# Channel products of all mixers in float32r passes, outputs of six mixers by ScalarE and GpSimd

## The chip, the cores and the metric

The kernel runs on one core of a Trainium2 chip. The time is the device time of one execution in microseconds, a median of several; the profiled execution is one more, with its own time. PE is TensorE, DVE VectorE, ACT ScalarE, POOL GpSimd, SP the SyncE queue that issues the DMAs.

## The reference

Eight batches, eight heads of 64, 576 tokens. Attention keeps the 32 largest scores of each row; its output x (576 tokens by 512 channels) goes through a mixer with a channel product at its end.

```python
scores = scale * np.matmul(q, k.transpose(0, 1, 3, 2))
kth = np.partition(scores, -top_k, axis=-1)[..., -top_k:-top_k + 1]
scores = np.where(scores >= kth, scores, -1000000000.0)
attn = softmax(scores)                  # written out in the original
x = np.matmul(attn, v)                  # heads laid side by side: 512 channels
theta = x @ w_theta
zr, zi = x * np.cos(theta), x * np.sin(theta)
y = np.einsum('ts,bsd->btd', w_tok_r, zr) + np.einsum('ts,bsd->btd', w_tok_i, zi)
u = x + y
out = u + np.maximum(u @ w_ch, 0.0)
```

## The kernel before

**Attention.** The work is cut into 160 units: 8 batches, 4 pairs of heads, and per pair five blocks of queries (four of 128 tokens and a rest of 64, whose two heads share one tile). `scores` makes a unit's scores on PE (ps_score, L260; for full blocks the high and low float32r halves of k against a stacked q) and copies them by ACT into a buffer e (L269). `fold`, `pick` and `threshold` find the 32nd largest of 576 by DVE alone, with maxima of eight and replacements (L296 to L330); POOL keeps marks (L307, L333) and makes the limits (lim, L331). `penalize` is an ACT Relu into pen (L350) and a POOL subtraction (L352), `exponent` an ACT exponential (L362), `turn` PE transposes (pt L377, pq L387) with ACT copies out of PSUM (L379), `mix_values` the product with v (px, L407 and L410), `keep_values` an ACT copy into xt (L419).

**Mixer.** Each batch then has a mixer, a generator: normalization and transposes of x, theta (pth, L540), cosine and sine on ACT with POOL products (L567, L572) into tile z, then the two products that matter here. For each of 4 blocks of 128 channels and 2 halves of 288 tokens, nine token products are added up (py, L656) and DVE adds them to xt (`settle`, L632), which is then u. After that, for each of 4 blocks and 2 halves, four channel products (po, L688: `w_ch` tiles against u, plain float32, two PE instructions each), and `give` (L637) has DVE write max(po, 0) + u into the output block ot, which has one buffer (bufs=1, shared with a tile of the trigonometric part); after the second half SP stores it. Tile z has one buffer too, and so the next mixer's z waits until it is free.

**Passes.** A float32r tile holds the high part of a float32; the rest is kept in a second tile. `halve` makes both (ACT copy L423, subtraction L424 on the engine that it is given), and `passes` lists three products: high by high, high by low, low by high. The last mixer (batch 7, `split`) makes all its products in this way. The mixer of batch 6 (`parts`) does it for its channel products alone: its weights are halved by `halve_weights("ch")` (subtraction on DVE), u into tiles u_hi and u_lo (subtraction on DVE).

**Order.** `pipeline` writes the units one after the other, the steps of a unit in the order of the string PTUFKSTVMXZ, with scores three units ahead. The mixer of a batch runs beside the units of the next: `advance` lets its generator go on by a budget per unit, and each `yield` says what the piece before it cost (1 for a token or a float32 channel product). The last mixer has no units beside it. Instructions of an engine run in the order that the scheduler of the framework gives, with priorities from `later` and `high_priority`.

**Weights.** `widen_steps` turns the weights, given as 64-bit words, into float32, one job in each unit from the third on (step "M"): SP loads, three ACT operations, POOL products (L158, L160, L161). There are 17 jobs; the four of w_ch come last. The temporaries lie in the buffer of z (`room`). The pair of q and k after next is halved at the end of each pair of heads (POOL L213) and laid out by 12 SP copies.

## Time and profile before

| | |
|---|---|
| median of 3 runs | 1202.73 us (1202.6 to 1203.58) |
| profiled execution | 1202.05 us, its span 1200.3 us |
| granted TensorE clock, mean | 0.971 of full speed |
| busy PE / DVE / ACT / POOL | 1104.9 / 1102.9 / 1007.0 / 704.4 us |

The profile is of one execution. The span runs from its first to its last instruction; what lies around it is 1.75 us. A page gives shares and groups for the whole span; the chain of work that ended last tells which engine set the pace at each time, and windows cut busy times out of a stretch. A share of busy time is a mean over stages with different limits, so the rows below are taken from the stages in which the changed instructions stand.

### The profile page before, as it was taken

The page shows a single profiled execution, that of the slowest core. Times are in us where ns is not written, and L with a number is a line of the kernel's source. Part 1 is how long each engine was busy: PE and PEld are TensorE (multiplying, and loading weights), DVE is VectorE, ACT ScalarE, POOL GpSimd, SP SyncE. Part 2 cuts the span into 40 slices and gives each one's busy share as a digit, 9 for nine tenths or more (in the row PEclk, how much of TensorE's full clock was granted, in tenths as well). Part 3 has the DMA queues.
Part 4 walks back from the last instruction along what each step waited for, and adds up shares of the span by engine and source line. Part 5 has one row for each costly group of instructions (what it writes and reads, how often), then busy time and mean ns, then how long its engine had stood idle before and what let it go on. Part 6 is the DMA issues. An engine that isn't in the chain of part 4 may idle for free.

```text
span 1200.3 us, 23013 instructions
## 1 busy us (share of the span) xinstructions
PE 1104.9 (92%) x6325; PEld 839.3 (70%) x6325; DVE 1102.9 (92%) x4997; ACT 1007.0 (84%) x2029; POOL 704.4 (59%) x975
## 2 busy tenths in 40 slices
PE   4577768999999999999999999999999999999997
PEld 3454555777767876678757877677767777677887
DVE  7999999999999999999999999999999999997352
ACT  6899999998699988898798987899888987898560
POOL 5999765665365644666465653765545654656540
PEclk9867899999999999999999999999999999999999
DMA  6654432433432234332431334333332334200101
GB/s 172 189 165 129 118 82 73 101 92 81 132 80 71 58 107 112 100 93 71 125 94 46 81 102 121 76 96 90 95 91 69 92 102 122 72 13 7 41 1 43
DMA packets 80235, 108.24 MB, mean 90 GB/s; under 512 B 23136, under 2 KB 41824, under 8 KB 80096
## 3 DMA queue, kind: packets, MB, share of 16 engines
q1 hardware_dynamic: 80096, 106.67, 33.7%
q8 instruction: 53, 0.87, 0.3%
q14 instruction: 86, 0.70, 0.2%
HBM read 38.40 MB, written 9.44 MB: 40 GB/s over the span
## 4 chain that ended last, share of the span: by engine, by line
PE 49%; DVE 24%; ACT 17%; POOL 5%; issue 2%; DMA 2%; SPq 1%; ACTq 0%; DVEq 0%; POOLq 0%
PE py L656 15%; PE ps_score L260 6%; PE po L688 6%; PE pt L377 6%; PE px L407 6%; DVE lst L326 5%; PE pth L540 5%; DVE best L320 5%; DVE lst L304 4%; ACT e L362 4%; ACT pen L350 3%; ACT e L269 3%; DVE lo L297 2%; PE px L410 1%; DVE ps_score L296 1%
## 5 line engine op out<-in xcount | busy, mean ns | idle before, releaser
L352 POOL TENSOR_TENSOR e<-e,pen 128x576 f32<-128x576 f32 x288 | 366.3, 1287 | 105.1 <-ACT pen L350 104.0
L320 DVE MAX8 best<-lst 128x8 f32<-128x102 f32 (+3 forms) x1152 | 284.4, 288 | 8.4 <-POOL lim L331 7.8
L656 PE MATMUL py<-w,z 128*128 128x288 f32 x1008 | 267.9, 407 | 0.3 <-ACT xt L419 0.3
L362 ACT ACTIVATE e<-e,lim 128x576 f32<-128x576 f32 x288 | 225.1, 783 | 18.0 <-POOL e L352 17.2
L326 DVE MATCH_REPLACE8 lst<-best,lst 128x122 f32<-128x122 f32 (+2 forms) x864 | 231.4, 274 | 0.1
L350 ACT ACTIVATE pen<-e,lim 128x576 bf16<-128x576 f32 x288 | 210.3, 774 | 16.8 <-POOL lim L331 15.4
L260 PE MATMUL ps_score<-kh,q 128*128 128x288 f32 x512 | 184.5, 375 | 42.9 <-ACT e L269 21.9
L304 DVE MAX8 lst<-lo 128x8 f32<-128x72 f32 (+1 forms) x864 | 210.0, 294 | 0.1
L656 PEld LDWEIGHTS py<-w,z 128*128 128x128 f32 x1008 | 181.1, 191 | 40.2 <-ACT xt L419 1.2
L377 PE MATMUL pt<-ident,e 128*128 128x128 f32 x1152 | 181.0, 283 | 23.0 <-ACT e L362 14.9
L377 PEld LDWEIGHTS pt<-ident,e 128*128 128x128 f32 x1152 | 139.9, 144 | 63.4 <-ACT e L362 20.3
L269 ACT COPY e<-ps_score 128x576 f32<-128x576 f32 x256 | 161.8, 641 | 15.2 <-PE ps_score L260 14.7
L379 ACT COPY at<-pt 128x512 f32<-128x512 f32 x256 | 148.0, 586 | 16.1 <-PE pt L377 14.8
L260 PE MATMUL ps_score<-kl,q 128*128 128x288 f32 x512 | 150.7, 309 | 0.1
L407 PE MATMUL px<-at,vt 128*64 128x320 f32 (+1 forms) x1024 | 145.1, 428 | 1.7 <-ACT at L382 1.3
L260 PEld LDWEIGHTS ps_score<-kh,q 128*128 128x128 f32 x512 | 102.6, 200 | 62.4 <-ACT e L269 29.2
L297 DVE TENSOR_TENSOR lo<-ps_score,e 128x576 f32<-128x576 f32 (+1 forms) x160 | 109.9, 687 | 0.0
L407 PEld LDWEIGHTS px<-at,vt 128*64 128x64 f32 x1024 | 70.8, 143 | 55.5 <-issue 10.2
L260 PEld LDWEIGHTS ps_score<-kl,q 128*128 128x128 f32 x512 | 103.4, 202 | 6.7 <-issue 2.4
L540 PE MATMUL pth<-w,xt 128*128 128x512 f32 x224 | 103.2, 600 | 1.6 <-ACT xt L518 1.6
L213 POOL TENSOR_TENSOR raw<-raw,hi 128x1152 fp32r<-128x1152 f32 x31 | 82.1, 2649 | 31.8 <-ACT hi L212 28.1
L688 PE MATMUL po<-xt,w 128*128 128x288 f32 x384 | 100.4, 408 | 0.0
(138 smaller groups left out, 1918.0 us busy)
## 6 DMA issues: line engine op xcount, KB each, us to landing
kh<-hi SPq DMA_DIRECT2D x124, 144.0 KB, 2.8
kl<-raw SPq DMA_DIRECT2D x124, 144.0 KB, 2.7
raw<-in_qT_dram SPq DMA_DIRECT2D x31, 288.0 KB, 2.9
raw<-in_kT_dram SPq DMA_DIRECT2D x31, 288.0 KB, 3.2
q<-hi SPq DMA_DIRECT2D x62, 144.0 KB, 2.6
q<-raw SPq DMA_DIRECT2D x62, 144.0 KB, 2.8
vt<-in_v_dram SPq DMA_DIRECT2D x32, 256.0 KB, 3.3
out_dram<-ot SPq DMA_DIRECT2D x28, 288.0 KB, 2.2
```

The costliest lines, as they stand in the source:

```text
L260: nc.tensor.matmul(out[:, at : at + n], l, r, start=(i == 0), stop=(i == len(mm) - 1), skip_group_check=True)
L269: nc.scalar.copy(u.x[:, :, keys], u.ps[:, :, :HS])
L304: nc.vector.max(u.lst[:, w, QS + i * 8 : QS + i * 8 + 8], u.lo1[:, w, lo:hi])
L320: nc.vector.max(top[:, w, best], part[w])
L326: nc.vector.match_replace(out=rest, in_to_replace=top[:, w, best], in_values=part[w], imm_value=LOWEST)
L350: nc.scalar.activation(pen[:, w], u.x[:, w], AF.Relu, bias=u.lim[:, w, 0:1], scale=-STEEP)
L352: nc.gpsimd.tensor_sub(u.x[:, w], u.x[:, w], pen[:, w])
L362: nc.scalar.activation(u.x[:, w], u.x[:, w], AF.Exp, bias=u.lim[:, w, 1:2], scale=SCALE, accum_out=acc)
L377: fixed(nc.tensor.transpose(pt[:, c], e[:, w, at0 : at0 + P], ident))
L407: nc.tensor.matmul(px[sl, :n], pr["vt"][:, kb, sl], pr["at"][:, a, kb], start=(kb == 0), stop=False, skip_group_check=True)
L656: fill(nc.tensor.matmul(py[:, :HS], l, r, start=(i == 0), stop=(i == len(mm) - 1)))
L688: nc.tensor.matmul(po[:, :HS], l, r, start=(i == 0), stop=(i == len(mm) - 1))
```

## The change

It has four parts. Line numbers are those of the kernel before; the changed kernel's are some 13 to 31 higher (L688 becomes L719, L637 becomes L657 on ACT, L658 on POOL and L660 on DVE, L424 becomes L441, L352 becomes L369, L331 becomes L348, L158, L160 and L161 become L161, L163 and, for the channel weights, L167, L213 becomes L230).

1. The four channel weight tiles hold float32r high parts. `widen_steps` makes them by an ACT cast and takes the low part on POOL, and stores it by SP to a block in DRAM, `ch_low`, one job after.
2. The mixers of batches 0 to 6 make their channel products in passes. When all token products are written, u is cast into high parts on ACT and low parts on POOL, four blocks of 128x576 each, in a tile `halves` in the buffer of z; it is free when the last token product has read z. The low parts of the weights come by DMA from `ch_low`, 256 KB per block of 128 channels, into two places of that same tile: two loads ahead, the third and fourth when PE has finished the block that held the place. After the halving the generator yields 4, and 0.75 for every three passes. In the first block the last quarter of both halves' products comes at the end.
3. For batches 0 to 5 `give` becomes an ACT Relu from PSUM to ot and a POOL addition of u.
4. The last mixer loads the low parts of the channel weights too, in place of halving them; the subtractions of `halve_weights` are all on POOL.

```diff
@@ pools @@
+    away = ctx.enter_context(tc.tile_pool(name="away", bufs=1, space=bass.MemoryType.DRAM))
...
@@ widen_steps @@
-        for key, n, width in (("ch", NB, DM), ("th", NB, DM), ("tok", KB, S)):
-            wts[key] = [weight_tile(F32, width) for _ in range(n)]
+        for key, n, width, dtype in (("ch", NB, DM, F32R), ("th", NB, DM, F32), ("tok", KB, S, F32)):
+            wts[key] = [weight_tile(dtype, width) for _ in range(n)]
+        ch_low[0] = away.tile([NB, P, NB, P], F32, tag="ch", name="ch_low")
...
             nc.gpsimd.tensor_add(low, low, bits)
+            if dst.dtype == F32R:
+                c = i - (len(jobs) - NB)
+                whole = bits.bitcast(F32)
+                nc.gpsimd.tensor_mul(whole, low.bitcast(F32), sign)
+                halve(dst, whole, whole, nc.scalar.copy, nc.gpsimd.tensor_sub)
+                return lambda: nc.sync.dma_start(
+                    ch_low[0][:, :, c].rearrange("m p d -> p m d"), whole.rearrange("p (m d) -> p m d", d=P)
+                )
             nc.gpsimd.tensor_mul(dst, low.bitcast(F32), sign)
...
+        store = None
         for i in range(len(jobs)):
             if i + 1 < len(jobs):
                 fetch(i + 1)
-            convert(i)
+            done = convert(i)
+            if store:
+                store()
+            store = done
             yield
+        store()
+        yield
...
@@ halve_weights @@
-            halve(hi[c], lo[c], wts[key][c], nc.scalar.copy, nc.vector.tensor_sub if key == "ch" else nc.gpsimd.tensor_sub)
+            halve(hi[c], lo[c], wts[key][c], nc.scalar.copy, nc.gpsimd.tensor_sub)
...
@@ mixer @@
         if split:
             halve_weights("tok")
+            flat = two_blocks("e", NB, DM, "c_lo", EBUFS)
+            c_lo = [t.rearrange("p (k d) -> p k d", d=P) for t in flat]
+            for m in range(NB):
+                nc.sync.dma_start(c_lo[m].bitcast(F32), ch_low[0][m])
...
         def give(m, c, cs, ot, y):
-            nc.vector.scalar_tensor_tensor(ot[:, cs], y, 0.0, xt[:, m, cs], op0=ALU.max, op1=ALU.add)
+            if beside and bq < B - 2:
+                nc.scalar.activation(ot[:, cs], y, AF.Relu)
+                nc.gpsimd.tensor_add(ot[:, cs], ot[:, cs], xt[:, m, cs])
+            else:
+                nc.vector.scalar_tensor_tensor(ot[:, cs], y, 0.0, xt[:, m, cs], op0=ALU.max, op1=ALU.add)
...
-        if parts:
-            halve_weights("ch")
-            u_hi, u_lo = two_blocks("kh", NB, S, "u_hi"), two_blocks("q2", NB, S, "u_lo")
-            for p in range(NB):
-                halve(u_hi[p], u_lo[p], xt[:, p], nc.scalar.copy, nc.vector.tensor_sub)
+        if not split:
+            room = one.tile([P, ZB * DM], F32R, tag="z", name="halves")
+            u_hi, u_lo = [[room[:, (2 * m + i) * S : (2 * m + i + 1) * S] for m in range(NB)] for i in range(2)]
+            flat = [room[:, 2 * NB * S + i * DM : 2 * NB * S + i * DM + DM] for i in range(TEMPS)]
+            c_lo = [flat[m % TEMPS].rearrange("p (k d) -> p k d", d=P) for m in range(NB)]
+            for m in range(TEMPS):
+                nc.sync.dma_start(c_lo[m].bitcast(F32), ch_low[0][m])
+            for m in range(NB):
+                halve(u_hi[m], u_lo[m], xt[:, m], nc.scalar.copy, nc.gpsimd.tensor_sub)
+            yield 4
...
+            heads = ((0, range(NB)), (1, range(NB)))
+            if m == 0 and not split:
+                heads = ((0, range(NB - 1)), (1, range(NB - 1)), (0, (NB - 1,)), (1, (NB - 1,)))
+            for c, kbs in heads:
...
-                else:
-                    mm = [(wts["ch"][kb][:, ms], xt[:, kb, cs]) for kb in range(NB)]
...
+                for kb in kbs:
+                    mm = passes(wts["ch"][kb][:, ms], c_lo[m][:, kb], u_hi[kb][:, cs], u_lo[kb][:, cs])
+                    for i, (l, r) in enumerate(mm):
+                        pos = dict(start=(kb == 0 and i == 0), stop=(kb == NB - 1 and i == 2), skip_group_check=True)
+                        with later(M_TOK if split else 0):
+                            nc.tensor.matmul(po[:, :HS], l, r, **pos)
                     if not split:
-                        yield NB / len(mm)
+                        yield 0.75
                         flush()
...
+            if not split and m + TEMPS < NB:
+                nc.sync.dma_start(c_lo[m + TEMPS].bitcast(F32), ch_low[0][m + TEMPS])
```

**TensorE, first mixer, from the last token product to the channel products.** Names: ps_score are scores of the running units, pt and pq their transposes, px their products with v. Before, the first channel products follow on score products:

```order
L260 MATMUL ps_score<-kh,q_3115 128x288
L260 MATMUL ps_score<-kl,q_3115 128x288
L688 MATMUL po<-xt,w_236 128x288
L688 MATMUL po<-xt,w_237 128x288
L688 MATMUL po<-xt,w_238 128x288
L688 MATMUL po<-xt,w_239 128x288
L387 MATMUL pq<-ident,e 128x128 x2
L688 MATMUL po<-xt,w_236 128x288
L688 MATMUL po<-xt,w_237 128x288
L688 MATMUL po<-xt,w_238 128x288
L688 MATMUL po<-xt,w_239 128x288
L377 MATMUL pt<-ident,e 128x128 x4
```

After:

```order
L277 MATMUL ps_score<-kl,qpad_100 128x64
L404 MATMUL pq<-ident,e 128x128 x2
L719 MATMUL po<-halves,w_238 128x288 x2
L719 MATMUL po<-halves 128x288
L719 MATMUL po<-halves,w_239 128x288
L424 MATMUL px<-at_3322,vt 64x256 x8
L394 MATMUL pt<-ident,e 128x128 x4
L719 MATMUL po<-halves,w_239 128x288
L719 MATMUL po<-halves 128x288
L719 MATMUL po<-halves,w_240 128x288 x2
L719 MATMUL po<-halves 128x288
L719 MATMUL po<-halves,w_241 128x288
```

Each product with a float32 weight tile has become three with halves, and score products, transposes and px of the running units stand between them in other places. Between the last py and the first po there are now 17 score products, a set of four transposes (pt) and two single ones (pq).

**GpSimd, in the first mixer's channel products.** lim, marks and e are of the running units' thresholds and penalties. Before:

```order
L307 COPY marks<-lst 128x2x3
L331 TENSOR_TENSOR lim<-best,factors 128x4
L352 TENSOR_TENSOR e<-e,pen 128x576 x2
L333 COPY marks<-best 128x2x4
L331 TENSOR_TENSOR lim<-best,factors 128x4
L352 TENSOR_TENSOR e<-e,pen 128x576 x2
L307 COPY marks<-lst 128x2x3
L333 COPY marks<-best 128x2x4
```

After:

```order
L441 TENSOR_TENSOR halves<-xt,halves 128x576 x3
L350 COPY marks<-best 128x2x4
L369 TENSOR_TENSOR e<-e,pen 128x576
L348 TENSOR_TENSOR lim<-best,factors 128x4
L369 TENSOR_TENSOR e<-e,pen 128x576
L441 TENSOR_TENSOR halves<-xt,halves 128x576
L369 TENSOR_TENSOR e<-e,pen 128x576 x2
L324 COPY marks<-lst 128x2x3
L324 COPY marks<-lst 128x3
L658 TENSOR_TENSOR ot<-ot,xt 128x288 x4
L350 COPY marks<-best 128x2x4
L324 COPY marks<-lst 128x2x3
```

The four remainders of u stand among the units' work, and the additions of two output blocks (four halves) stand in a row ahead of the next unit's limits.

**GpSimd, at the start, where the channel weights are widened.** room holds the widening's temporaries, w_... are weight tiles, raw and hi the pair that is halved. Before, around the first two of the four blocks:

```order
L352 TENSOR_TENSOR e<-e,pen 128x576
L333 COPY marks<-best 128x2x4
L161 TENSOR_TENSOR w_236<-room 128x512
L158 TENSOR_TENSOR room<-room,eight 128x512
L307 COPY marks<-lst 128x2x3
L331 TENSOR_TENSOR lim<-best,factors 128x4
L160 TENSOR_TENSOR room<-room 128x512
L352 TENSOR_TENSOR e<-e,pen 128x576 x2
L333 COPY marks<-best 128x4
L161 TENSOR_TENSOR w_237<-room 128x512
L158 TENSOR_TENSOR room<-room,eight 128x512
```

After, around the remainders of the first two blocks:

```order
L163 TENSOR_TENSOR room<-room 128x512
L369 TENSOR_TENSOR e<-e,pen 128x576 x2
L350 COPY marks<-best 128x4
L441 TENSOR_TENSOR room<-room,w_238 128x512
L167 TENSOR_TENSOR room<-room 128x512
L230 TENSOR_TENSOR raw<-raw,hi 128x1152
L324 COPY marks<-lst 128x2x3
L350 COPY marks<-best 128x2x4
L348 TENSOR_TENSOR lim<-best,factors 128x2
L369 TENSOR_TENSOR e<-e,pen 128x576 x2
L441 TENSOR_TENSOR room<-room,w_239 128x512
```

A block's last product (L161 before) is now L167, and the remainder L441 has been added behind it; two of these stand ahead of and behind the pair's subtraction (L230).

## Rows read from the trace of the kernel before

**Rows 1.** The page, shares of busy time by engine and the span in 40 equal slices (30 us each; a digit is the busy share of a slice in tenths).

```profile
PE 1104.9 (92%) x6325; PEld 839.3 (70%) x6325; DVE 1102.9 (92%) x4997; ACT 1007.0 (84%) x2029; POOL 704.4 (59%) x975
...
PE   4577768999999999999999999999999999999997
...
DVE  7999999999999999999999999999999999997352
```

**Rows 2.** The page, the chain of work that ended last: shares of the span by engine, then by line.

```profile
PE 49%; DVE 24%; ACT 17%; POOL 5%; issue 2%; DMA 2%; SPq 1%; ACTq 0%; DVEq 0%; POOLq 0%
PE py L656 15%; PE ps_score L260 6%; PE po L688 6%; PE pt L377 6%; PE px L407 6%; DVE lst L326 5%; PE pth L540 5%; DVE best L320 5%; DVE lst L304 4%; ACT e L362 4%; ACT pen L350 3%; ACT e L269 3%; DVE lo L297 2%; PE px L410 1%; DVE ps_score L296 1%
```

**Rows 3.** The chain in order of time, from 1040 us to the end, where the last two mixers run; columns: start us, us, engine, tile and line, count of instructions.

```profile
1116.04 1.60 PE po L688 x12
...
1118.07 1.58 PE po L688 x12
...
1180.58 12.72 PE po L688 x96
```

**Rows 4.** The chain in order of time from 284 to 326 us, in the product stage of the first mixer (same columns); the first and the last of its eight groups of po, and one row of each of other products between them.

```profile
291.05 1.94 PE po L688 x8
...
302.14 0.53 PE ps_score L260 x4
...
305.57 0.22 PE pq L387 x2
...
314.62 1.94 PE po L688 x8
...
317.09 0.44 PE pt L377 x4
```

**Rows 5.** The chain in order of time from 425 to 462 us, in the product stage of the second mixer (same columns); the first and the last of the eight rows of ot.

```profile
433.01 0.36 DVE ot L637
...
454.53 0.36 DVE ot L637
```

**Rows 6.** Windows: stretch, its us, busy us of PE, PEld, DVE, ACT and POOL with the number of instructions, the clock granted to TensorE, the DMA share and GB/s. The first two lie in the widening at the start, the others around the product stages of the mixers of batches 0, 1, 4 and 5, four of six such windows; the two left out lie between these in every column of busy time.

```profile
90.00:120.00 30.00, 21.68 (x107) 14.88 (x103) 28.99 (x150) 27.20 (x55) 28.39 (x36) 0.73 0.45 129
120.00:150.00 30.00, 23.00 (x121) 16.02 (x122) 27.80 (x133) 27.62 (x59) 23.37 (x31) 0.81 0.46 118
290.00:324.00 34.00, 33.97 (x207) 27.50 (x207) 33.48 (x144) 27.46 (x56) 16.24 (x23) 1.00 0.35 100
430.00:464.00 34.00, 33.90 (x211) 26.71 (x209) 33.97 (x153) 28.84 (x60) 17.88 (x27) 1.00 0.43 118
...
830.00:864.00 34.00, 34.00 (x198) 27.02 (x197) 33.72 (x158) 26.75 (x56) 16.30 (x30) 1.00 0.37 103
970.00:1004.00 34.00, 34.00 (x200) 27.03 (x199) 33.28 (x157) 26.85 (x55) 17.44 (x29) 1.00 0.43 118
```

**Rows 7.** Groups of instructions by line with shapes kept apart: line, engine, operation, out<-in, shape, count | busy us, mean ns of one | idle time of the engine before them. The last line is from the view of one tile, u_lo: ns of one (least, median, most), first and last start.

```profile
L269 ACT COPY e<-ps_score 128x576 f32<-128x576 f32 x256 | 161.8, 641 | 15.2 <-PE ps_score L260 14.7
...
L567 POOL TENSOR_TENSOR z<-z 128x512 f32<-128x512 f32 x32 | 41.1, 1286 | 52.9 <-ACT z L566 49.6 <-DVE lo L299 3.2
...
L419 ACT COPY xt<-px 128x320 f32<-128x320 f32 x32 | 13.6, 424 | 12.5 <-PE px L410 12.5
...
L424 POOL TENSOR_TENSOR w<-w,w_hi 128x576 fp32r<-128x576 f32 x9 | 12.9, 1433 | 4.9 <-ACT w_hi L423 4.3
...
L419 ACT COPY xt<-px 128x256 f32<-128x256 f32 x32 | 11.6, 364 | 4.3 <-PE px L410 3.8
...
L572 POOL TENSOR_TENSOR whole<-end,whole 128x256 f32<-128x256 f32 x7 | 5.1, 732 | 2.4 <-ACT whole L564 2.4
...
L423 ACT CAST w_hi<-w 128x512 fp32r<-128x512 f32 x8 | 4.6, 624 | 0.2 <-PE pq L387 0.2
...
L423 ACT CAST u_hi<-xt 128x576 fp32r<-128x576 f32 x4 | 2.7, 666 | 0.0
...
L424 POOL TENSOR_TENSOR w_lo<-w,w_hi 128x512 fp32r<-128x512 f32 x1 | 1.3, 1305 | 0.1
...
L424 DVE TENSOR_TENSOR u_lo<-xt,u_hi x4: 734/748/759, 1068.5 to 1109.5; 128x576 fp32r<-128x576 f32 x4
```

**Rows 8.** The chain in order of time from 86 to 130 us (columns as in rows 3), where the channel weights are widened.

```profile
118.63 2.38 POOL raw L213
...
121.19 4.82 DMA room<-in_w_ch_dram
...
126.68 0.65 ACT room L157
127.33 0.53 ACT e L269
...
127.89 0.47 DVE ps_score L296
```

**Rows 9.** The page's DMA issues (out<-in, queue, count, KB each, median us from issue to landing), and one line of the view of waits (who waits <- for whom: us in all, times, longest us).

```profile
vt<-in_v_dram SPq DMA_DIRECT2D x32, 256.0 KB, 3.3
out_dram<-ot SPq DMA_DIRECT2D x28, 288.0 KB, 2.2
...
DVE ot L637 <- DMA out_dram<-ot: 7.1, 3, 2.6
```

More of the change, by code (lines that the diff above doesn't have):

```diff
@@ L116, in topk_attention_phase_mixer @@
     wts = {}
+    ch_low = [None]
     def weight_tile(dtype, width):
@@ L459, in share, with mixer @@
         return pace[0]
-    def mixer(bt, split=False, beside=False, parts=False):
+    def mixer(bt, split=False, beside=False):
         bq, xt, sums, sums_rem = bt["bq"], bt["xt"], bt["sums"], bt["sums_rem"]
@@ L762, in keep @@
                         done = B - 1 - u.bq
-                        running.append(mixer(u.batch, done == 0, done > 0, done == 1))
+                        running.append(mixer(u.batch, done == 0, done > 0))
             def ahead():
```

23 lines of the change are left out of this document (9 added, 14 removed).

## The prediction

> **What bounds the kernel now.** I read the shares of busy time and the slices first, then the chain of work that ended last, then windows of the stages that the change touches, then prices of single operations. The page shows two engines full at once: PE and DVE are both busy for 92% of the span and stand at nine tenths in nearly every slice between the start and the tail [rows 1]. So a gain needs both to get less work in the same stretch, and the chain has to say which of the two sets the pace where.
>
> By line, the chain gives the channel products (po, L688) 6%, some 72 us of 1200.3 [rows 2]. Of these, 2 x 12.7 = 25.4 us belong to the last two mixers, which already work in float32r passes (96 in 12.72 us [rows 3]). That leaves about 47 us for the six other mixers, and one such mixer's products are 8 groups of 1.94 us = 15.5 us [rows 4]. Three mixers make 46.6 us. So in three of the six mixers with float32 products PE is the chain through the whole product stage, as [rows 4] shows for the first; in the other three the chain runs through DVE, and there the operation that adds the output up (ot, L637) is on it with 0.36 us each time [rows 5]. The six windows of 34 us around the product stages say how little is between the two: PE is busy 33.9 to 34.0 us, DVE 33.3 to 34.0, ACT 26.8 to 28.8, POOL 16.2 to 17.9 [rows 6]. The clock granted to PE there is 1.00, so nothing hangs on it.
>
> **Channel products in passes.** A float32 product of 128x288 is two instructions; one accumulation of four products takes 1.94 us [rows 4]. The same accumulation in passes is 12 instructions, and 12 of them take 1.58 to 1.60 us in the seventh mixer [rows 3]; 96 in 12.72 us is 1.59 for 12. One group saves 1.94 - 1.59 = 0.35 us, a mixer with its 8 groups 2.8 us, six mixers 16.8 us of PE. On the chain only three mixers count: 3 x 8 x 0.35 = **-8.4 us**. The seventh mixer and the last keep their passes: 0.
>
> The rows make twelve passes 0.82 of the eight instructions. The Trainium skill (FP8 and Floating Point Precision, section TensorE Precision Notes) says that a true fp32 product is four passes through the array; three of four would be 0.75, 0.485 us a group, 11.6 us instead of 8.4, and would put the sum below at 1190.5 us. The rows decide here, as they hold the weight loads too.
>
> **Outputs by ScalarE and GpSimd.** DVE loses 8 operations in each of six mixers, at 0.36 us of its time each [rows 5]; in the three mixers where DVE is the chain this is 3 x 8 x 0.36 = **-8.6 us**. In the other three it is what lets the gain of PE stand: DVE there has 0.3 to 0.7 us to spare in a window [rows 6] and would be the bound at once if it kept them. ACT gains 8 operations of 128x288 per mixer; its copies out of PSUM take 364 ns at 256 columns and 424 at 320 [rows 7], so 0.39 us, 3.1 us a mixer. POOL gains 8 adds of 128x288; 732 ns at 256 columns and 1286 at 512 [rows 7] give about 0.80 us, 6.4 us a mixer.
>
> **Halving the moving operand.** Each of the first seven mixers now casts four blocks of 128x576 on ACT (666 ns, 2.7 us a mixer) and takes four remainders on POOL (1433 ns, 5.7 us a mixer) [rows 7]. The seventh mixer had both before, the remainders on DVE, and in addition halved the weights of the channel product once (4 x 0.62 us on ACT); what DVE loses there lies in the tail, where PE is the chain [rows 3], and counts 0. The remainder on DVE took 748 ns, on POOL 1433 [rows 7]. The Trainium skill (GPSIMD Engine Reference, section 4.1 Engine selection) advises VectorE for a two-input add, as GpSimd is about twice as slow; the rows agree (1.9 times). By that rule alone the outputs would stay on DVE, and the term of 8.6 us would fall away.
>
> **What the product stage then needs.** A window of 34 us should shrink to about 34 - 2.8 = 31.2 us. POOL needs 17 + 5.7 + 6.4 = 29 us of it. ACT needs 27.5 + 3.1 + 2.7 = 33.3 us by durations, but these overlap when work is dense: the copy of L269 lasts 641 ns [rows 7] and costs 0.53 on the chain [rows 8]. With 0.1 us off each of 56 old and 12 new operations ACT needs 26.5 us. So PE, DVE, ACT and POOL would all be 85 to 107% full. Bounds per mixer: nothing lost (ACT 26.5), or all but 0.7 us lost (ACT 33.3, so 2.1 us). Then there is the new wait at the start of the stage: the halves lie in the buffer of z, so the casts wait until the last product of py is done, then come a cast, a remainder and the load of the low weights (256 KB; the values of that size land after 3.3 us [rows 9]). Between the last py and the first po the order puts 17 score products, a set of transposes and two single ones, 17 x 0.13 + 0.44 + 0.22 = 2.9 us of PE by the steps of [rows 4]; the first remainder is there after some 0.7 + 1.4 us of work plus queueing, so PE waits 0 to 3 us. What waits behind PE's first product is the transposes and values of the running unit. I take 0.8 us a mixer for the stage and its start together, near the lower end, since ACT falls below the new window at the middle of its bounds (29.9 us): six mixers **+5 us**, bounds 0 and 17. For the seventh mixer, in the tail, the same start wait counts 0, since the casts stand beside px products and transposes of the last units; if that cover is gone it is up to 3 us.
>
> **Widening the weights at the start.** The four blocks of the channel weights get a cast on ACT (about 0.62 us) and a remainder on POOL (1305 ns [rows 7]) and a store each. Here POOL is busy 28.4 of 30 us between 90 and 120 us, then 23.4 of 30 [rows 6], and the chain runs on POOL until 121 us, then through the last load of these weights, ACT and DVE [rows 8]. In the order, two of the four remainders stand ahead of POOL's work for the pair and its subtractions there, two after it: 2 x 1.3 = 2.6 us on the chain, and the stores stand in SP's queue ahead of the pair's copies. I take **+3 us**, bounds 0 and 6 (all four, and ACT's casts).
>
> **DMA queue.** SP issues four loads and waits for PE with two of them; behind these stand the loads of a later pair and the outputs. The outputs already land 2.2 us after issue [rows 9]; these loads are ahead of their use by more than a unit, so I count 0 beyond the wait named above.
>
> **Sum.** The profiled execution took 1202.05 us (span 1200.3 and 1.75 around it); the median of the runs shown is 0.7 higher. -8.4 - 8.6 + 3 + 5 = -9.0 us: 1193.0 for an execution like the profiled one, **1193.7 us** as a median.
>
> **Rivals.**
> 1. Everything fits: ACT's operations overlap as its old ones do, the start waits are covered, POOL's extra work at the start falls into its idle 6.6 us. Then the whole 17 us come: 1185.7 us. For it: POOL has half of each product window free. Against it: ACT is at 80% of that window already.
> 2. ACT becomes the bound of the product stage without waiting: 33.3 us in place of 34, six times -0.7, plus 3 at the start: about 1201.5 us, no change that can be told (0.2%, 2.4 us, is about what a measurement of this kernel can tell).
> 3. Slower: the output block has one buffer, so ACT's Relu of the next block waits until the former block is added and has left. Two adds (1.6 us), an issue and 2.2 us to landing are about 4.1 us; in the order the third block's Relu stands three ACT operations (some 1.5 us) behind the second's, and POOL's adds stand ahead of a unit's limits and subtractions, so score copies, penalties and exponentials queue up behind them. PE needs 2 x 1.59 us for the products between and some 0.2 for what stands among them, 3.4 us, which leaves 0.7 us of waiting. With ACT at 33.3 us and two such waits a window is 34.7 us, six times +0.7, plus 3: 1210 us. It decides from about 0.7 us of waits at full durations, or 4 us at the middle ones. For it: DVE already met this wait three times, 7.1 us in all [rows 9].
> That the passes are not made is no rival: their pitch is in [rows 3].
>
> **Chances.** The forecast (1188 to 1200) 0.53, rival 1 (below 1188) 0.17, rival 2 0.13, rival 3 0.17. Faster by over 0.2%: 0.53 + 0.17 = 0.70; within it 0.13; slower 0.17. The range 1185 to 1207 leaves out about one in ten above (the dear half of rival 3) and some 5 in 100 below.
>
> **What would show it.** Right: twelve po passes in 1.6 us and no DVE operation of ot in the first six mixers; product windows some 2 us shorter; ACT and POOL at nine tenths there; the end of the widening some 3 us later. Wrong: PE or DVE waiting for ACT's score copies in the product stage for more than 2 us a mixer, Relu waiting for the output DMA, PE idle before the first po for more than 1 us a mixer, or the first mixer starting as early as before.

## The result and the profile after

The changed kernel takes 1208.59 us (median of 7 runs, 1207.01 to 1211.13) against 1202.6 us before (7 runs, 1199.83 to 1204.15): a ratio of 1.0057, 95% interval 1.0048 to 1.0067. It is slower by 6 us. The forecast was 1193.7, and the range ended at 1207.

The profiled execution after took 1211.13 us (span 1209.3), the slowest of the seven; the comparison below goes against the 1202.05 us of the profile before. The shares of the page answer to [rows 1] and the shares of the chain to [rows 2]:

```profile
PE 1103.1 (91%) x6517; PEld 849.5 (70%) x6517; DVE 1083.4 (90%) x4941; ACT 1032.5 (85%) x2101; POOL 780.7 (65%) x1055
...
PE 57%; ACT 16%; DVE 14%; DMA 6%; issue 3%; POOL 3%; SPq 1%; ACTq 0%; POOLq 0%; DVEq 0%
PE py L679 20%; PE ps_score L277 7%; PE pt L394 7%; PE px L424 7%; PE pth L555 5%; PE po L719 5%; DVE lst L343 3%; DVE best L337 3%; ACT pen L367 2%; DVE lst L321 2%; ACT e L379 2%; ACT e L286 2%; PE px L427 2%; DVE lo L314 1%; DMA halves<-ch_low 1%
```

DVE has lost 19.5 us of work; ACT has gained 25.5, POOL 76.3. What is new on the chain is DMA, 6% where it was 2%.

Where the time went is read from the token products, whose line names its first and last start. Of before and of after:

```profile
L656 PE MATMUL py<-w,z x1008: 403/406/511, 223.5 to 1106.6; 128*128 128x288 f32 x168
```

```profile
L679 PE MATMUL py<-w,z x1008: 403/406/510, 230.3 to 1112.0; 128*128 128x288 f32 x168
```

The first token product is 6.8 us late. From there I cut the span at each mixer's first token product: the **start** (up to the first of batch 0), the **loop** (six cycles, from there to the first of batch 6) and the **tail** (from there to the end of the last channel product). These are times of the timeline of PE, subtracted:

| us | start | loop | tail |
|---|---|---|---|
| before | 223.5 | 825.0 | 144.8 |
| after | 230.3 | 824.6 | 148.5 |

So the start lost 6.8 us, the loop gained 0.4 where 12 were forecast, and the tail lost 3.7; behind the last product 1.1 came back. The sum is 9.0, the difference of the spans.

**The loop.** Four windows of 34 us around product stages, batches 0, 1, 4 and 5, answer to [rows 6]:

```profile
297.00:331.00 34.00, 33.36 (x248) 28.30 (x247) 31.72 (x144) 28.51 (x62) 25.39 (x33) 1.00 0.44 133
435.00:469.00 34.00, 30.93 (x229) 26.46 (x230) 31.77 (x139) 30.07 (x67) 26.27 (x35) 1.00 0.47 136
848.00:882.00 34.00, 32.04 (x238) 27.52 (x238) 31.23 (x136) 29.27 (x63) 27.01 (x34) 1.00 0.44 127
986.00:1020.00 34.00, 32.84 (x251) 28.66 (x251) 32.21 (x151) 30.73 (x67) 27.75 (x37) 1.00 0.51 141
```

PE and DVE, both full before, now stand idle for 0.6 to 3.1 and 1.8 to 2.8 us, and ACT and POOL are not full either (28.5 to 30.7 and 25.4 to 27.8 of 34). Nobody is the bound: somebody waits. DVE waits for ACT's score copies, 21.7 us in the loop against 7.6 before (view of waits, 230 to 1045 us), a sign that the prediction had named. What ACT and PE wait for, the chain of the third mixer's product stage says, in order of time (start us, us, what):

```profile
572.76 2.89 DMA halves<-ch_low
...
585.01 3.17 PE po L719 x24
...
590.26 0.81 POOL ot L658
...
591.21 0.76 POOL ot L658
...
591.99 2.10 DMA out_dram<-ot
...
594.17 0.29 ACT ot L657
...
596.65 1.06 ACT hi L229
...
597.73 0.49 SPq L242
...
598.31 2.95 DMA out_dram<-ot
...
601.34 0.42 ACT ot L657
601.76 0.04 issue
601.81 2.37 PE px L424 x16
```

Twelve passes take 1.59 us (24 in 3.17), as [rows 3] said. Behind them stands a chain that was not there before: two additions on POOL, the store, its landing, and only then the next Relu, because ot has one buffer. The second time the store comes later still: on SP it stands behind a copy of the next pair, which waits for ACT's cast of that pair (596.65, then SP's queue at 597.73), and takes 2.95 us. The two additions of that block had ended at 597.35 (timeline of POOL), the store went out at 598.31. The Relu at 601.34 frees the accumulators, which px shares with po, and px of the running unit starts at once. The direct waits are small; the view of waits (us in all, times, longest):

```profile
POOL ot L658 <- ACT ot L657: 15.3, 8, 3.1
...
DVE ot L660 <- DMA out_dram<-ot: 7.0, 3, 2.5
...
ACT ot L657 <- DMA out_dram<-ot: 5.3, 5, 2.1
...
PE po L719 <- DMA halves<-ch_low: 4.1, 5, 1.3
```

The Relu's waits for the store lie in the mixers of batches 0, 2 and 4 alone (at 313 to 318, 594 to 601 and 869 to 877 us in the timeline of ACT); the chain runs through a store in the stages of batches 2 and 4. In the other three mixers no Relu waits for it. The wait for the first load of low weights is there in all six, 0.1 to 1.3 us of PE each. Before the change no output of the loop waited for the block: the three waits of [rows 9] lie in the tail, the first of them here.

```profile
1117.26 0.88 DVE L637 SCALAR_TENSOR_TENSOR ot<-po,xt 128x288 f32<-128x288 f32 x2 [2.64 <-DMA out_dram<-ot]
```

**The start.** The chain from 100 us on, which answers to [rows 8]:

```profile
121.83 8.56 DMA q<-raw
...
131.04 2.47 DMA ch_low<-room
...
133.60 0.69 ACT room L160
```

The copy of the pair lands 8.56 us after its issue. On SP the first store of low weights (120.61) and a load of raw weights (121.24) went out just ahead of it. Before, the copies were issued at the same time, with the load ahead of them but no store, and this copy landed after 4.7 us. Then a second store is on the chain, for which ACT's next widening waits.

That is not all of it. PE's four sets of sixteen products with v (px from at and vt) that started at 154.5, 167.8, 182.9 and 209.1 us before now start 3.8, 2.9, 4.5 and 7.4 us later. The delay grows in a stretch in which TensorE had a lower granted clock than before, and there the second set took 3.96 us in place of 2.37. A window, and that set in PE's timeline, of before and of after:

```profile
170.00:190.00 20.00, 15.76 (x88) 11.26 (x87) 20.00 (x92) 18.62 (x38) 13.88 (x18) 0.91 0.44 104
...
167.82 2.37 PE L407 MATMUL px<-at,vt 128*64 128x320 f32 x16 [0.64 <-ACT at L382]
```

```profile
170.00:190.00 20.00, 16.06 (x82) 10.69 (x83) 19.91 (x95) 18.52 (x40) 13.20 (x20) 0.74 0.36 85
...
170.74 3.96 PE L424 MATMUL px<-at,vt 128*64 128x320 f32 x16 [1.84 <-ACT at L399]
```

In this window the granted clock is 0.69 to 0.76 in the profiles of all six kernels that halve and store in the widening (the changed one, passes_alone, start_alone, tail_dve, tail_own, out_in_xt) and 0.83 to 0.94 in those of the other eleven. That the lower clock makes up the rest of the 6.8 us is not shown; it stands where the rest arises.

**The tail.** The seventh mixer's remainders (halves) stand in turn with POOL's halving of the last mixer's weights (w), all behind the last token product at 1112.0; the first channel product comes at 1116.25, and at 1124 the last quarter of the first block still waits for the last remainder:

```profile
1115.97 1.36 POOL halves L441
1117.33 1.38 POOL w L441
1118.70 2.75 POOL halves L441 x2
1121.45 1.25 POOL w L441
1122.70 1.39 POOL halves L441
1124.09 0.04 issue
1124.14 0.55 PE po L719 x2
```

### The profile page after: what moved, and what is told of

It reads as the page before. It is cut to its first block, busy times and chain, and to the rows that moved or that the text cites. A ratio compares the mean times of both kernels' runs of the same rounds, so it can differ in the third digit from the quotient of the medians.

```text
span 1209.3 us, 23519 instructions
## 1 busy us (share of the span) xinstructions
PE 1103.1 (91%) x6517; PEld 849.5 (70%) x6517; DVE 1083.4 (90%) x4941; ACT 1032.5 (85%) x2101; POOL 780.7 (65%) x1055
## 4 chain that ended last, share of the span: by engine, by line
PE 57%; ACT 16%; DVE 14%; DMA 6%; issue 3%; POOL 3%; SPq 1%; ACTq 0%; POOLq 0%; DVEq 0%
PE py L679 20%; PE ps_score L277 7%; PE pt L394 7%; PE px L424 7%; PE pth L555 5%; PE po L719 5%; DVE lst L343 3%; DVE best L337 3%; ACT pen L367 2%; DVE lst L321 2%; ACT e L379 2%; ACT e L286 2%; PE px L427 2%; DVE lo L314 1%; DMA halves<-ch_low 1%
## 5 line engine op out<-in xcount | busy, mean ns | idle before, releaser
L369 POOL TENSOR_TENSOR e<-e,pen 128x576 f32<-128x576 f32 x288 | 367.3, 1289 | 107.0 <-ACT pen L367 102.7
L277 PE MATMUL ps_score<-kl,q 128*128 128x288 f32 x512 | 153.2, 313 | 0.5 <-DMA kl<-raw 0.4
L424 PE MATMUL px<-at,vt 128*64 128x320 f32 (+1 forms) x1024 | 148.0, 428 | 5.1 <-ACT at L399 2.9
L424 PEld LDWEIGHTS px<-at,vt 128*64 128x64 f32 x1024 | 70.9, 142 | 61.3 <-issue 11.2
L719 PE MATMUL po<-halves,w 128*128 128x288 f32 x448 | 96.9, 304 | 2.9 <-POOL halves L441 1.9
L313 DVE TENSOR_TENSOR ps_score<-ps_score,e 128x288 f32<-128x288 f32 (+1 forms) x160 | 68.1, 426 | 33.3 <-ACT e L286 28.5
```

The lines of the kernel that those rows point to most:

```text
L277: nc.tensor.matmul(out[:, at : at + n], l, r, start=(i == 0), stop=(i == len(mm) - 1), skip_group_check=True)
L369: nc.gpsimd.tensor_sub(u.x[:, w], u.x[:, w], pen[:, w])
L424: nc.tensor.matmul(px[sl, :n], pr["vt"][:, kb, sl], pr["at"][:, a, kb], start=(kb == 0), stop=False, skip_group_check=True)
```

## The experiments

Every median stands with its ratio to the kernel before, taken in the same series, and the 95% interval. The table after them has start, loop and tail of each.

**Each part alone.** `gives_alone` is the kernel before with part 3 only:

```diff
+            if beside and bq < B - 2:
+                nc.scalar.activation(ot[:, cs], y, AF.Relu)
+                nc.gpsimd.tensor_add(ot[:, cs], ot[:, cs], xt[:, m, cs])
+            else:
                 nc.vector.scalar_tensor_tensor(ot[:, cs], y, 0.0, xt[:, m, cs], op0=ALU.max, op1=ALU.add)
```

> The kernel before with part 3 alone: Relu by ScalarE and addition by GpSimd for batches 0 to 5, float32 channel products, no halving. Theory A (the single output block makes the Relu wait for addition and landing, and the accumulators are held that long): PE needs two groups of 1.94 us and little else per block against a chain of two additions and a landing of about 4 us, so PE waits a little in most blocks: 1203 to 1208 us. Rival B (what hurts is how full ScalarE and GpSimd are, and they are not so full without the halving): 1200 to 1203 us, as DVE loses 8.6 us on the chain of three mixers, of which PE gives back most.

Measured: 1210.05 us, 1.0069 (1.0055 to 1.0084). Slower by itself, with float32 products and without the halving of six mixers. Beyond A's range, but on its side; the mechanism of A is not shown by it, as the trace has 1.6 us of Relus waiting for the store (three waits), and its loop is 7.5 us longer than before.

`passes_alone` is the changed kernel with all outputs by DVE:

```diff
-            if beside and bq < B - 2:
+            if False:
```

> The changed kernel with its outputs by VectorE as before: passes, halving, loads and the wider start stay. Theory A (start +6.8 us and tail +4.7 us are separate from the outputs; in the loop the wait for the first loads stays, the wait for the output block goes, and VectorE is the bound again): 1206 to 1211 us. Rival B (the outputs on ScalarE and GpSimd are the main cost): 1203 us or below.

Measured: 1219.54 us, 1.0157 (1.0134 to 1.0179). Neither. In the loop either half alone is worse than both: 832.5 us with the outputs, 839.0 with the passes, 824.6 with both. (As a median gives_alone is not to be told from the changed kernel, since it has no loss in start and tail.) The outputs on ACT and POOL aren't the main cost; they are what makes the passes bearable.

`start_alone` is the kernel before with this behind the last product of the widening of each channel weight block (cut to the lines that matter), and the store one job later, as in the change:

```diff
+            c = i - (len(jobs) - NB)
+            if c >= 0:
...
+                part = bits.bitcast(F32)
+                halve(spare[0][:, c % 2, :DM], part, dst, nc.scalar.copy, nc.gpsimd.tensor_sub)
+                return lambda: nc.sync.dma_start(
+                    ch_low[0][:, :, c].rearrange("m p d -> p m d"), part.rearrange("p (m d) -> p m d", d=P)
+                )
```

> The kernel before with the start's part alone: after each of the four channel weight blocks is widened, its high part is cast by ScalarE (into a spare buffer that nothing reads), the remainder taken by GpSimd and stored by SP one job later; nothing else is changed and nothing reads what was stored. Theory A (the start costs what weights_later gave back in the first 230 us): first token product 5 to 7 us late, 1207 to 1210 us. Rival B (the start costs little, and weights_later gained by the order that the scheduler made of the loop): first token product within 2 us, 1201 to 1204 us.

Measured: 1208.61 us, 1.0052 (1.0039 to 1.0066). Its token products start at 230.0 us, 6.5 late, and end 8.1 late; from the third cycle on the loop has the old order and the old times. A holds; the start alone is worth as much as the whole loss. The path is another one than in the changed kernel: here the copy of the pair landed 2.8 us after its issue, and on the chain stood the last load of raw weights, which went out at 124.93, behind the copies, and landed 3.2 us later than before. So the late copy is one way for the start to lose, not the cause that both share.

```profile
L675 PE MATMUL py<-w,z x1008: 403/406/510, 230.0 to 1114.7; 128*128 128x288 f32 x168
```

**The start mended.** `weights_later` widens the channel weights as before the change, but into a buffer of the scores, and halves and stores them in the units after (cut):

```diff
-            if dst.dtype == F32R:
...
+        for _ in range(WLATE):
+            yield
+        for c in range(NB):
+            whole = jobs[c - NB][0]
+            halve(wts["ch"][c], whole, whole, nc.scalar.copy, nc.gpsimd.tensor_sub)
+            nc.sync.dma_start(
+                ch_low[0][:, :, c].rearrange("m p d -> p m d"), whole.rearrange("p (m d) -> p m d", d=P)
+            )
+            yield
```

> The changed kernel with the four channel weight blocks widened as before (into a buffer of the scores) and halved in the units after, one per unit, so that the remainders and stores stand after the pair's subtraction and copies at 120 us. Theory A (the 6.8 us that the first token product is late come from these remainders and stores ahead of the pair's copies): 1202 to 1204 us, first token product at 224 to 226 us. Rival B (it is the amount of work of GpSimd and ScalarE ahead of the first mixer, wherever it stands): 1207 to 1209 us, first token product at 229 to 231 us.

Measured: 1198.51 us, 0.9974 (0.9962 to 0.9986), faster than before. The first token product is back at 224.6 us, as A said, but 10 us came and not 6: the loop, whose code is the same, is 9.8 us shorter as well. (5.7 and 9.8 are more than 10, as the profiled execution after was 2.5 us above its median and this one 2.9 below.) Its order differs from the changed kernel's in the first four cycles and is the same on every engine in the last two; most of the gain lies in the cycles of batches 1 and 2, which took 139.7 and 139.3 us after, 134.5 and 136.8 here. Its Relus wait 2.9 us for the store, in six waits of at most 0.7, where the changed kernel has 5.3 with 2.1 as the longest. What the one output block costs hangs on the order that the scheduler makes around it.

```profile
L681 PE MATMUL py<-w,z x1008: 403/406/510, 224.6 to 1096.6; 128*128 128x288 f32 x168
```

**The tail.** `tail_dve` puts the seventh mixer's four remainders back on DVE, nothing else:

```diff
-                halve(u_hi[m], u_lo[m], xt[:, m], nc.scalar.copy, nc.gpsimd.tensor_sub)
+                halve(u_hi[m], u_lo[m], xt[:, m], nc.scalar.copy, nc.gpsimd.tensor_sub if beside and bq < B - 2 else nc.vector.tensor_sub)
```

> The changed kernel with the four remainders of the seventh mixer's u on VectorE, as before the change; batches 0 to 5 keep GpSimd. Theory A (in the tail the remainders queue behind GpSimd's halving of the last mixer's weights and the first channel product waits for them, 7 us of which 4.7 stay to the end): 1204 to 1205 us. Rival B (the first products wait for the loads and for the casts as well, so that only the order of the waits changes): 1207 to 1209 us.

Measured: 1212.77 us, 1.0087 (1.0072 to 1.0101). Both theories fell: the tail grew by 8 us. The four subtractions took 12.75 us on DVE, beside POOL's halving of weights (ns of one: least, median, most; then the four in DVE's timeline and three of the subtractions in POOL's):

```profile
L441 DVE TENSOR_TENSOR halves<-xt,halves x4: 1765/1896/7421, 1110.0 to 1115.4; 128x576 fp32r<-128x576 f32 x4
...
1110.05 12.75 DVE L441 TENSOR_TENSOR halves<-xt,halves 128x576 fp32r<-128x576 f32 x4 [1.95 <-ACT halves L440]
...
1118.22 3.96 POOL L441 TENSOR_TENSOR w<-w,w_hi 128x576 fp32r<-128x576 f32 x3
```

`tail_own` gives that mixer's halves their old buffers and its remainders to DVE, and loads its low weights ahead of the token products (cut):

```diff
+        tail = beside and bq == B - 2
+        if tail:
+            flat = two_blocks("e", NB, DM, "early", EBUFS)
...
+        if tail:
+            u_hi, u_lo = two_blocks("kh", NB, S, "u_hi"), two_blocks("q2", NB, S, "u_lo")
+            for p in range(NB):
+                halve(u_hi[p], u_lo[p], xt[:, p], nc.scalar.copy, nc.vector.tensor_sub)
```

> The changed kernel with the seventh mixer's halves of u in buffers of their own (those of the pairs, as before the change), its remainders on VectorE, and its low weights loaded into buffers of the scores ahead of its token products; batches 0 to 5 and the start stay as in the change. Theory A (in the tail the casts, remainders and loads all stand behind the last token product because the halves share z, and this costs 7 us there): first channel product of that mixer within 1 us of the last token product, and 1203 to 1205 us. Rival B (the tail loses to something else, such as the loads of the last mixer or GpSimd): 1207 to 1210 us.

Measured: 1206.66 us, 1.0032 (1.0020 to 1.0045), between the two. The wait ahead of the products is gone (the first starts 3.2 us before the last token product ends, by the timeline of PE), but the tail still takes 148.1 us. `later_tail` has the edits of weights_later and of tail_own, as they stand above:

> The edits of weights_later and tail_own together. Theory A (start and tail are separate costs that add up): 1198.5 - 4 to 5 = 1193 to 1195 us. Rival B (whatever is gained in the tail is met by other waits there): 1197 to 1199 us.

Measured: 1197.68 us, 0.9959 (0.9946 to 0.9972); its interval overlaps that of weights_later. B: the tail keeps its loss.

**The output block.** `out_in_xt` is the changed kernel with two lines changed. With passes, u is read only as halves once they are made, so POOL adds in place and SP stores from xt; ot is free after the addition:

```diff
-                nc.gpsimd.tensor_add(ot[:, cs], ot[:, cs], xt[:, m, cs])
+                nc.gpsimd.tensor_add(xt[:, m, cs], ot[:, cs], xt[:, m, cs])
...
-                nc.sync.dma_start(outT[bq, m * P : m * P + P], ot)
+                nc.sync.dma_start(outT[bq, m * P : m * P + P], xt[:, m] if beside and bq < B - 2 else ot)
```

> The changed kernel with one edit: for batches 0 to 5 GpSimd adds into xt in place and SP stores from xt (start and tail as in the change). Theory A (the wait for the one output block is a cost of the change itself, about 6 us as between later_tail and later_tail_xt): 1201 to 1204 us. Rival B (it only pays in the order that the loop has with the later weights): 1207 to 1210 us.

Measured: 1194.59 us, 0.9935 (0.9922 to 0.9948): 14 us off the changed kernel, more than twice what A expected. The six cycles take 811.3 us, all between 134.0 and 136.0. No Relu waits for a store any more. In the third mixer's stage the Relus (timeline of ACT) now follow the products more closely: the last product of the stage ends at 590.20, the last two Relus start at 590.58 and 592.30. In the changed kernel the last product ended at 598.29 and both came from 601.34 on.

```profile
577.06 0.73 ACT L657 ACTIVATE ot<-po 128x288 f32<-128x288 f32 x2
...
580.97 0.81 ACT L657 ACTIVATE ot<-po 128x288 f32<-128x288 f32 x2
...
584.11 0.41 ACT L657 ACTIVATE ot<-po 128x288 f32<-128x288 f32 x1 [0.54 <-PE po L719]
585.64 0.41 ACT L657 ACTIVATE ot<-po 128x288 f32<-128x288 f32 x1 [1.13 <-PE po L719]
...
590.58 0.42 ACT L657 ACTIVATE ot<-po 128x288 f32<-128x288 f32 x1
...
592.30 0.42 ACT L657 ACTIVATE ot<-po 128x288 f32<-128x288 f32 x1
```

The changed kernel's, of the second half of that stage:

```profile
594.17 0.71 ACT L657 ACTIVATE ot<-po 128x288 f32<-128x288 f32 x2 [0.44 <-DMA out_dram<-ot]
...
601.34 0.71 ACT L657 ACTIVATE ot<-po 128x288 f32<-128x288 f32 x2 [0.65 <-DMA out_dram<-ot]
```

The edit changed the order in every cycle, and so it doesn't show the wait by itself. The cycles, by the batch whose mixer opens them:

| us | 0 | 1 | 2 | 3 | 4 | 5 |
|---|---|---|---|---|---|---|
| after | 137.3 | 139.7 | 139.3 | 135.6 | 137.8 | 134.9 |
| out_in_xt | 136.0 | 135.1 | 135.3 | 135.5 | 135.3 | 134.0 |

The cycles of batches 0, 2 and 4, in which the Relus had waited for the store, gained 7.8 us together; those of 1, 3 and 5, in which none had, gained 5.6.

`later_tail_xt` makes the same edit in later_tail:

> As later_tail, but for batches 0 to 5 GpSimd adds into xt in place and SP stores from xt, so the output block is free for the next Relu after the addition and not after the store has landed. Theory A (the wait for the store, 2 to 3 us twice on the chain of each product stage, holds the accumulators and so PE): 1190 to 1195 us. Rival B (ScalarE's queue is what delays the Relu, not the block): within 2 us of later_tail, 1196 to 1200 us.

Measured: 1191.59 us, 0.9910 (0.9895 to 0.9926), the best version: 10 us below the kernel before. A holds, but here the edit is worth 6 us (3.6 in the loop) and not 14. Its product windows of batches 4 and 5 (34 us, as above) are full again, for PE and DVE both:

```profile
837.00:871.00 34.00, 33.65 (x247) 28.46 (x248) 33.46 (x147) 30.19 (x66) 25.89 (x36) 1.00 0.48 133
973.00:1007.00 34.00, 34.00 (x248) 28.62 (x245) 33.70 (x152) 30.97 (x68) 26.42 (x37) 1.00 0.49 140
```

**Passes with DVE's outputs, start and tail mended.** `later_tail_passes` is later_tail with `if False:` as in passes_alone; `passes_xt` in addition lets DVE write into xt in every mixer but the last:

```diff
-                nc.vector.scalar_tensor_tensor(ot[:, cs], y, 0.0, xt[:, m, cs], op0=ALU.max, op1=ALU.add)
+                o = ot[:, cs] if split else xt[:, m, cs]
+                nc.vector.scalar_tensor_tensor(o, y, 0.0, xt[:, m, cs], op0=ALU.max, op1=ALU.add)
```

> As later_tail, with the outputs of batches 0 to 5 on VectorE, so passes alone with start and tail mended. Theory A (passes and outputs are worth something only together, since PE and VectorE are both full: with VectorE's outputs kept the loop is paced by VectorE): 1200 to 1206 us. Rival B (the two parts add up, 8.4 us by the passes and 8.6 by the outputs): 1194 to 1197 us, at most 3 us above later_tail.

Measured: 1217.55 us, 1.0124 (1.0109 to 1.0138), far beyond A and B.

> As later_tail_passes (outputs by VectorE), with VectorE writing each output into xt in place and SP storing from xt. Theory A (passes alone are slow because VectorE, full already, waits for the one output block in a product stage that has become shorter): 1198 to 1206 us. Rival B (VectorE's work itself, 8 operations per mixer in a stage that PE would now leave earlier, or the order made for it): 1213 to 1220 us.

Measured: 1208.40 us, 1.0049 (1.0035 to 1.0062), between A and B. Freeing the block gives 9 of the 20 us to later_tail, the new order included. Without the block's wait passes alone leave the loop where it was before (824.8 against 825.0 us): what PE gains, less what the halving costs, is worth nothing while DVE keeps its outputs.

**Loads ahead.** `later_tail_early` loads the first two blocks of low weights of each mixer into a buffer of the scores while the last token products run:

```diff
+            if m == NB - 1 and not split and not tail:
+                early = wk2.tile([P, 2, S], F32R, tag="e", name="early", bufs=EBUFS)
+                for i in range(TEMPS):
+                    nc.sync.dma_start(
+                        early[:, i, :DM].bitcast(F32).rearrange("p (k d) -> p k d", d=P), ch_low[0][i]
+                    )
```

> As later_tail, and the first two blocks of low weights of batches 0 to 5 are loaded into a buffer of the scores while the last token products run, the other two into the place of z at once. Theory A (the wait for the first loads costs each of six mixers some 1 to 2 us of PE): 4 to 8 us below later_tail. Rival B (the casts and remainders of u, which stay behind the last token product, end last anyway, or PE has other work there): within 2 us of later_tail.

Measured: 1219.35 us, 1.0140 (1.0118 to 1.0161). Both theories missed by some 20 us or more. DVE waited 53.1 us in all for ACT's score copies, against 26.4 in later_tail. The buffer is one of the eleven that scores live in; whether that or the other order did it was not tried apart.

**The pace of the mixer.** `later_tail_paced` is later_tail and `passes_paced` later_tail_passes with another count for three passes; `xt_fast` is later_tail_xt with 0.625 in the same place:

```diff
-                        yield 0.75
+                        yield 0.875
```

> As later_tail with the same budget of 0.875 for three passes. Theory A (pace matters): 3 us or more from later_tail, to either side. Rival B: within 2 us of later_tail.

Measured: 1216.19 us, 1.0119 (1.0103 to 1.0134). A holds.

> As later_tail_passes (outputs by VectorE), but three passes count 0.875 in the budget of the running mixer and not 0.75, so that a mixer's products fill 104 counts as before and not 100. Theory A (passes alone lose 15 us because the product stage is done too early against the units, and theta with its waits comes where VectorE is behind): 1202 to 1208 us. Rival B (VectorE sets the pace of that stage whatever the pace of the mixer): 1214 to 1220 us.

Measured: 1226.04 us, 1.0195 (1.0177 to 1.0213). Neither: it got slower still.

> As later_tail_xt, with 0.625 in place of 0.75 for three passes in the budget of the running mixer, so that the product stage is over earlier against the units. Theory A (the longer product stage at 0.875 was the loss of 18 us, and the same slope goes on): 1186 to 1190 us. Rival B (0.75 is the share of PE's time that three passes have beside a float32 product, 0.40 to 0.485 us or 0.82, so a smaller count makes the stage too dense for PE): 1192 us or more.

Measured: 1205.08 us, 1.0028 (1.0019 to 1.0036). B holds by its number. Of the three counts tried 0.75 is the best, and 0.125 off it costs 8 to 19 us; the way this goes was not settled.

| us | start | loop | tail | median |
|---|---|---|---|---|
| gives_alone | 222.2 | 832.5 | 145.0 | 1210.05 |
| passes_alone | 229.1 | 839.0 | 147.6 | 1219.54 |
| start_alone | 230.0 | 826.6 | 144.9 | 1208.61 |
| weights_later | 224.6 | 814.8 | 148.5 | 1198.51 |
| tail_dve | 228.7 | 821.4 | 156.8 | 1212.77 |
| tail_own | 228.3 | 822.9 | 148.1 | 1206.66 |
| later_tail | 225.9 | 814.5 | 148.5 | 1197.68 |
| out_in_xt | 229.7 | 811.3 | 148.4 | 1194.59 |
| later_tail_xt | 226.4 | 810.9 | 147.2 | 1191.59 |
| later_tail_passes | 226.4 | 836.9 | 147.4 | 1217.55 |
| passes_xt | 227.2 | 824.8 | 148.5 | 1208.40 |
| later_tail_early | 224.9 | 838.3 | 149.0 | 1219.35 |
| later_tail_paced | 225.5 | 834.7 | 148.4 | 1216.19 |
| passes_paced | 226.3 | 845.7 | 146.2 | 1226.04 |
| xt_fast | 224.9 | 823.8 | 147.4 | 1205.08 |

The parts are of one profiled execution each, cut as above. The changed kernel, tail_dve and tail_own have one order up to the end of the fifth cycle, and their loops took 824.6, 821.4 and 822.9 us: differences of up to 3 us say little here.

## Why the prediction was wrong

In the profiled executions 9.0 us came on top where 9.0 were to go. Of these 18 us the loop is 11.6, the start 3.8 and the tail 3.7; 1.1 came back at the end.

**The gains, when the block is free.** Twelve passes cost 1.59 us, as the rows had it, not three quarters of eight instructions. The two terms, -8.4 and -8.6 us, can be tested only as a pair: with the output in xt the loop is at 824.8 us with passes alone and at 811.3 or 810.9 with both, against 825.0 before. So the sentence that the one lets the other stand was right, and 14 us of the 17 are there. PE's waits for the first loads, which the term for the stage had counted, are 4.7 us in out_in_xt, close to the 5 that were taken; the two terms by themselves were not measured.

**The step that failed is "What the product stage then needs".** Taken at +5 us with bounds of 0 and 17, it measured 16.6 (the 17 that were to come, less the 0.4 that came). It priced ACT and POOL by how full they are, and they never became full; a wait for the output block stood in it at nothing and was left to rival 3, with a chance of 0.17. What the runs showed in its place is that wait, the Relu for the one output block and PE for the accumulators that the Relu holds, and the order that the scheduler made around it. The two lines of out_in_xt that free the block earlier take 13.3 us off the loop: 7.8 in the three cycles with the wait, 5.6 in the three without, where only the order can have done it. With the block kept, weights_later has another order and a loop that is 9.8 us shorter, and freeing the block takes 3.6 more (later_tail to later_tail_xt). So the block and the order share the 13.3 us, and the shares hang on each other; the forecast had priced neither.

Rival 3 came near with its 1210 us, but by luck, as it was made of other parts: it had six windows 0.7 us longer and 3 us at the start, where the loop measured -0.4 us, the start +6.8 and the tail +3.7. It cited that DVE had met the wait before, but these waits lie in the tail. And it set two additions, an issue and a landing of 2.2 us (4.1 in all) against 3.4 us of PE's products, 0.7 us of waiting; on the chain the second store went out 0.96 us after its additions had ended, behind a pair's copy on SP, and took 2.95 us. "DMA queue: I count 0" is the sentence that missed this: it had the outputs behind the loads, but not behind the copies, which wait for ACT.

**The start** was taken at +3, with a bound of 6, and measured +6.8; start_alone has 6.5, and 8 us later on. POOL's remainders were priced, the four stores were named and given 0.4 us. With the halving later the start is at +1.1, so it is where this work stands that costs, and not how much it is; remainders and stores were not tried apart. The 3 us were near what the trace had by 168 us (2.9 to 3.8), and the rest arose where the granted clock was lower. The prediction looked at the clock of the product stages, where it is 1.00, and not here, where its own [rows 6] show 0.73 and 0.81.

**The tail** was counted 0, "since the casts stand beside px products and transposes"; "up to 3 us" was said for no cover, and 3.7 was measured. That halves, remainders and loads behind the last token product cause the late first product is shown by tail_own, which moved all three; that they cause the 3.7 us is not, as the tail kept 148.1 us without them. Part 4 of the change, by which the last mixer loads its low weights and POOL makes all remainders of the weights, is in every version whose tail is 146 us or more and in none at 145, and was not tried alone. What the tail's loss is stays open.

**Which engine.** The Trainium skill (GPSIMD Engine Reference, section 4.1 Engine selection) prices an add on GpSimd at about twice VectorE's; the rows agree again (1420 ns after against 748 before for a remainder). But the choice that follows from this price alone would be wrong by 17 us here for the outputs (passes_xt against later_tail_xt), since VectorE was full and GpSimd was not.

**Open** are the tail, the pace, the path of the start's loss, and how much of the loop's 13.3 us is the wait itself.

## What to carry to other kernels

When an operation moves from one engine to two in a row, follow its output buffer to the end: addition, place in the store queue, landing, and who holds what until then. A buffer that one engine could live with became a wait when two engines in a row shared it. Two engines that were both full gained only together here, so test such a change whole and each half alone; look whether an edit also changes the order that the scheduler makes, before you put its gain down to the wait that it removes; and look what a once-only piece of work at the start pushes back in the queues, since nothing later makes up for it.

## What was not expected of the hardware

A DVE subtraction of 128x576 that took 748 ns before took 1896 ns in the median and 7421 at most in tail_dve, while POOL ran subtractions of its own without a gap. Each of the four ended some 0.6 us after the end of a POOL operation; the longest, from 1115.38 us on, was out over five subtractions of POOL, with one small addition between them, the last of which ended at 1122.18, and it ended at 1122.80. The Trainium skill (SBUF — State Buffer, section Terms) says that VectorE and GpSimd share a pair of ports, that one instruction holds it to its end, and that the loser stands still; this trace agrees. In the kernel before, the same four subtractions kept 734 to 759 ns; two of them had no POOL operation beside them, and the other two overlapped with penalty subtractions of POOL only at their ends.
